# Attention and two feed-forward layers on one core: seven gelus on one engine, and a maximum over tokens in three operations

## The chip, the cores and the metric

The kernel runs on one core of a Trainium2 chip. The metric is the device time of one execution in microseconds (us). The engines are named as the profile names them: PE is TensorE (matmuls; PEld its weight loads), DVE is VectorE, ACT is ScalarE, POOL is GpSimd, SP is SyncE, which issues the DMAs. Differences of under about 2 us cannot be told from run to run (the three runs shown below spread over 1.45 us).

## What is computed

A linear attention with softmaxes over q's features and over k's tokens, then two feed-forward layers with different activations:

```python
q_s = softmax(q, axis=-1)                 # 4 batches, 8 heads, 576 tokens, 64 features
k_s = np.exp(k - np.max(k, axis=2, keepdims=True))
k_s = k_s / (np.sum(k_s, axis=2, keepdims=True) + 1e-09)
kv = np.einsum('bhsd,bhse->bhde', k_s, v)
x = np.einsum('bhsd,bhde->bhse', q_s, kv)  # -> 2304 tokens x 512
h = x @ w_in                               # 512 -> 2048
g = h * (1.0 / (1.0 + np.exp(-1.702 * h))) # the gelu of this text
x = g @ w_out                              # 2048 -> 512
h = x @ w_in2
out = (h * np.tanh(np.log1p(np.exp(h)))) @ w_out2
```

All matmuls of the feed-forward layers run in a 32-bit format that keeps fewer bits. So each operand is split into a high part (a copy in that format) and a low part (the value less the high part), and every product is made of three matmuls.

## The kernel before

**Tiles and stages.** Tokens come in five blocks (512, 512, 512, 384, 384). The first three blocks of the first layer run as 48 *units*, 16 to a block; unit n is one 128-wide slice of the 2048 hidden features of one block. A unit is 12 matmuls into one of two PSUM banks `h` (`gemm_in`, L938), the gelu (`gelu`, L952 and L957), the split into high and low parts (`gelu_split`, recorded at L352 and L344), and, two units later, 12 matmuls into the four banks `acc` (`gemm_out`, L981). PE's order in a quiet stretch is in(n), out(n-2), in(n+1), out(n-1), and so on. Behind unit 47 comes a second phase, which makes the rest of the first layer and the second layer with fewer, combined matmuls (L1203, L1456, L1561, L1586).

**What runs beside the units.** During block 0 (units 0 to 15) all 32 weight tiles of the first layer are still being made: each is loaded raw by a DMA, scaled twice (L361, on ACT), put together by three operations of DVE (L398, L405, L410), and split (L352, L344). `attention(blk)` makes the input x of a block: `q_soft` is the softmax of q, `k_later` and `k_kv` handle two heads of k and v at a time (four such k units for a batch of tokens), `q_turn` and `x_part` make x itself (L812 on ACT, L817 on DVE write it). `attention(0)` runs first and uses another path for k (`k_first`). `attention(1)` must be done before unit 16, `attention(2)` before unit 32, and `attention(3)`, which needs fresh k units as well, directly behind it. `attention(4)` has no k units.

**The gelu before.** ACT takes tanh(0.851 h) from PSUM into `gt` (L952); DVE adds 1 and multiplies by h (L957), which gives twice the gelu. The bank h is free when L957 has read it. x2_evac multiplies by 0.5 later. Tanh and Exp are in the table of functions that ACT loads at the start (L312), and two more loads come in the second phase (L1224).

**The maximum over tokens before.** `k_max` takes the maximum of a tile of 96 partitions x 768 over its 6 tokens per partition with one reduction (L599), whose input is read with the token as the innermost index, so with a step of 64 elements. PE turns the result over (L603), DVE reduces the rest (L604), PE spreads it over partitions again (L677), DVE subtracts (L679), ACT takes Exp (L680), PE multiplies with v (L693), and ACT scales the result (L721).

**What sets the order.** The kernel first collects all operations with their reads and writes (`plan.op` with keys). A planner then orders them for every engine by urgency and by an estimated cost, and emits them; it also chooses the engine where two can do an operation (`either` is DVE or POOL, `copy` is DVE or ACT). Each engine then runs its own queue strictly in order, and waits for the others by semaphores. So a changed cost or dependency can change any order of the whole program.

Of the kernel before, what the change touches and what calls it, by code (L numbers as in the profile page):

```python
# [210 lines left out]
def tile_attention_moe_moe(  # L211
# [29 lines left out]
    SIZES = (512, 512, 512, 384, 384)  # L241
    NBLK = len(SIZES)
    NDIR = 3
    BEGIN = (None, 2, 18, 26, 34)
    BASE = [sum(SIZES[:t]) for t in range(NBLK + 1)]
    MB = max(SIZES)
    MH = max(SIZES[1::2])
# [40 lines left out]
    ap = actx.enter_context(tc.tile_pool(name="attn", bufs=1))  # L288
    kt = [ap.tile([KP, 2, KC, D], F32, name=f"kt{i}") for i in range(2)]
    qt = ap.tile([P, NCT, 4, D], F32, name="qt")  # L290
    pmt = [ap.tile([KP, P], F32, name=f"pmt{i}") for i in range(2)]
    kv32 = [ap.tile([P, P], F32, name=f"kv32_{i}") for i in range(NHP)]
    qT32 = [ap.tile([P, MB], F32, name=f"qT32_{i}") for i in range(2)]
    mcol = ap.tile([P, NHP], F32, name="mcol")
# [23 lines left out]
    def f32(t):  # L318
        return t.bitcast(F32)
# [10 lines left out]
    def pe(ns, reads, writes, fn, whole=False):  # L330
        plan.op([(PE, ns, fn, whole)], reads, writes)
# [258 lines left out]
    def k_max(u, ps, key):  # L590

        kk = ("kt", k_tile(u))
        t, m, mk = kt[k_tile(u)], mcol[:, u % NHP : u % NHP + 1], ("mc", u % NHP)
        pm, pk = pmt[u % 2], ("pm", u % 2)
        dve(
            768,
            [kk],
            [pk],
            lambda: nc.vector.reduce_max(  # L599
                out=pm.rearrange("p (j d) -> p j d", j=2), in_=t.rearrange("p j c d -> p j d c"), axis=AX.X  # L600
            ),
        )
        pe(110, [pk], [key], lambda: nc.tensor.transpose(ps, pm, ident[0:KP, 0:KP]))  # L603
        dve(96, [key], [mk], lambda: nc.vector.reduce_max(out=m, in_=ps, axis=AX.X))  # L604

    def k_first(u, ps, keys):
# [33 lines left out]
        for i, (lo, hi) in enumerate(TURNS):  # L640
            act(
                (hi - lo) * KP + 150,
                [keys[i], mk],
                [tk + (i,), sk + (i,)],
                lambda i=i, n=(hi - lo) * KP: nc.scalar.activation(
                    out=turned[i], in_=ps[i][:, 0:n], func=AF.Exp, bias=m, accum_out=ks[:, u, i : i + 1]
                ),
                psum=True,
            )
# [23 lines left out]
    def k_later(u, ps1, ps2, key):  # L673
        kk, mk = ("kt", k_tile(u)), ("mc", u % NHP)
        t, m = kt[k_tile(u)], mcol[:, u % NHP : u % NHP + 1]
        k_max(u, ps1[:, 0:KP], key)
        pe(110, [mk], [key], lambda: nc.tensor.transpose(ps2[0:KP, :], m.to_broadcast([P, KP]), ident))  # L677
        far = ps2[0:KP, :].rearrange("p (j o d) -> p j o d", j=2, o=1).to_broadcast([KP, 2, KC, D])
        dve(768, [kk, key], [kk], lambda: nc.vector.tensor_tensor(out=t, in0=t, in1=far, op=ALU.subtract))  # L679
        act(768, [kk], [kk], lambda: nc.scalar.activation(out=t, in_=t, func=AF.Exp))  # L680

    def k_kv(u, ps3, key3):
        first = u < NHP
# [64 lines left out]
    def q_soft(blk, half, begun):  # L748
# [20 lines left out]
        if (blk, half) in GROUPS:  # L769

            dve(NQ, [sk], [sk], lambda: nc.vector.tensor_single_scalar(out=s, in_=s, scalar=-1.0, op=ALU.mult))
            for i in range(NQ):
                act(
                    D + 223,
                    key + [sk],
                    key + [("qsum", half)],
                    lambda i=i: nc.scalar.activation(  # L777
                        out=flat()[:, i],
                        in_=flat()[:, i],
                        func=AF.Exp,  # L780
                        bias=s[:, i : i + 1],
                        accum_out=qsum[0:np_, half, i : i + 1],
                    ),
                )
            dve(NQ, [("qsum", half)], [sk], lambda: nc.vector.tensor_scalar_add(s, qsum[0:np_, half, :], 1e-9))
        else:
            either(n, ALU.subtract, flat, flat, wide, key + [sk], key)
            act(n, key, key, lambda: nc.scalar.activation(out=flat(), in_=flat(), func=AF.Exp))
            dve(n, key, [sk], lambda: nc.vector.reduce_sum(out=s, in_=flat(), axis=AX.X))
            dve(NQ, [sk], [sk], lambda: nc.vector.tensor_scalar_add(s, s, 1e-9))  # L790
        dve(8 * NQ, [sk], [sk], lambda: nc.vector.reciprocal(s, s))
# [140 lines left out]
    def gemm_in(h, hkeys, t, fc, ccs=range(NCC)):  # L932
        buf, nb = t % 2, SIZES[t]
        for cc in ccs:
# [10 lines left out]

            pe(3 * mm_ns(nb), x_keys(buf, cc) + [("W", 0, fc, 0), ("W", 0, fc, 1)], [spine] + hkeys, mm)

    def gelu(n):
        nb = SIZES[n // NFC]
        h = hps[n % 2][:, 0:nb]  # L950
        t, tk, hk = gt[n % 2][:, 0:nb], ("gt", n % 2), ("h", n % 2)
        act(nb, [hk, ("tables",)], [tk], lambda: nc.scalar.activation(out=t, in_=h, func=AF.Tanh, scale=0.851), psum=True)  # L952
        dve(
            nb,
# [5 lines left out]
    def gelu_split(n):  # L960
        nb = SIZES[n // NFC]
        t, tk = gt[n % 2][:, 0:nb], ("gt", n % 2)
        o = g_of(n)
        copy(nb, lambda: o[:, 0, :], lambda: t, [tk], [("g", n % 2, 0)])
        either(
            nb,
# [250 lines left out]
        return t.rearrange("p i a n -> p i (a n)")  # L1217

    def activated(n, j, half, t, tk):
        first = n in (0, NPR) and (j, half) == (0, 0)  # L1220

        def fn():
            if first:
# [454 lines left out]
    for n in range(NS):  # L1678
        t, fc = divmod(n, NFC)
        if n == 0:  # L1680

            gemm_in1(0, range(NCC // 2))
            gemm_in1(1, range(NCC // 2))
        gemm_in1(n, range(NCC) if n >= 2 else range(NCC // 2, NCC))
        gelu(n)
        if n >= 2:
            gemm_out(n - 2)
# [13 lines left out]
                x_split(kk, 0)  # L1701
        if n >= NS - 4 and n < NS:
            ring_load(0, n - NS + 4)
        if n in BEGIN:
            attention(BEGIN.index(n))
        if n == NS - 8:
            plan.op(
# [86 lines left out]
```

## Time and profile before

| | us |
|---|---|
| median of 3 runs | 835.64 |
| lowest and highest | 834.77, 836.22 |
| the profiled execution | 833.88 |
| its span, first to last instruction | 832.1 |

The profiled execution is 1.76 us under the median. PE is busy for 98% of the span, but that share is no measure of its pace: a matmul's record is longer than the step to the next one, and in a stretch with waits or with a lower clock PE looks nearly as busy. The pace is read from the chain of waits: in a quiet stretch 12 matmuls of 128x512 take 2.72 us. DVE and ACT records overlap their neighbours by about 0.08 to 0.1 us, so that the *step* from one to the next of a full engine is the recorded duration less that.

### The profile page before, as it was taken

To read this page: it belongs to the slowest core of one execution; us is meant where nothing else is said; L and a number is where in the kernel's file an instruction comes from. 1 tells how busy PE (TensorE), PEld (TensorE's weight loads), DVE (VectorE), ACT (ScalarE), POOL (GpSimd) and SP (SyncE) were. 2 spreads that over 40 slices of the span, in tenths; PEclk is the share of its full clock that TensorE was granted. 3 is DMA by queue.
4 is the path that set the end of the run, shared out by engine and by line. 5 is a ranking of instruction groups with operands and counts; after the bars stand their busy time and mean duration, and the time that the engine had idled before them with its cause. 6 is when DMAs were issued, how large, how long until landed. Compare 5 with 4: busy or idle time off the path is not lost.

```text
span 832.1 us, 13739 instructions
## 1 busy us (share of the span) xinstructions
PE 817.9 (98%) x4897; PEld 727.2 (87%) x4897; DVE 668.9 (80%) x1247; ACT 459.8 (55%) x916; POOL 17.9 (2%) x22
## 2 busy tenths in 40 slices
PE   8999989999999999999999999999999999999998
PEld 7787767887777887999999988988999999999998
DVE  7999996879998777764779979979587977777964
ACT  6988795335455444643447756448344555344542
POOL 0002100000000000000000000000000002000000
PEclk9999999999999999999999999999999999999999
DMA  9688771634468577766778888978788897588872
GB/s 265 193 247 256 212 233 51 207 115 130 135 198 262 201 241 256 211 220 221 249 240 307 270 256 252 276 233 254 232 289 277 277 367 281 181 263 274 289 240 58
DMA packets 120933, 191.75 MB, mean 230 GB/s; under 512 B 36897, under 2 KB 85281, under 8 KB 120865
## 3 DMA queue, kind: packets, MB, share of 16 engines
q1 hardware_dynamic: 120864, 190.88, 72.7%
q8 instruction: 39, 0.64, 0.3%
q14 instruction: 30, 0.24, 0.1%
HBM read 137.89 MB, written 52.95 MB: 229 GB/s over the span
## 4 chain that ended last, share of the span: by engine, by line
PE 82%; DVE 8%; ACT 4%; DMA 4%; issue 1%; SPq 1%; DVEq 0%; ACTq 0%
PE at L1203 21%; PE acc L1456 14%; PE acc L981 11%; PE h L938 10%; PE h L1203 7%; PE acc L1586 5%; PE acc L1561 5%; PE h L1586 3%; PE h L1561 3%; DMA raw<-in_moe_w_in_dram 1%; DMA raw<-in_moe_w_out_dram 1%; DVE pmt L599 1%; PE at L857 1%; DVE dec L410 1%; ACT qt L777 1%
## 5 line engine op out<-in xcount | busy, mean ns | idle before, releaser
L938 PE MATMUL h<-xt,wi 128*128 128x512 f32 x576 | 147.6, 399 | 1.4 <-DVE gt L957 0.9
L981 PE MATMUL acc<-g,wo 128*128 128x512 f32 x576 | 147.2, 400 | 0.4 <-ACT stage L801 0.4
L1203 PE MATMUL at<-xt,wi 128*128 128x384 f32 x732 | 144.4, 335 | 0.1
L1203 PEld LDWEIGHTS at<-xt,wi 128*128 128x128 f32 x732 | 128.8, 188 | 6.4 <-DVE quad L1255 0.4
L938 PEld LDWEIGHTS h<-xt,wi 128*128 128x128 f32 x576 | 106.0, 188 | 26.0 <-DVE gt L957 1.3
L981 PEld LDWEIGHTS acc<-g,wo 128*128 128x128 f32 x576 | 107.0, 189 | 24.0 <-ACT stage L801 0.8
L1456 PE MATMUL acc<-wi,second 128*128 128x256 f32 x738 | 91.0, 283 | 0.0
L1456 PEld LDWEIGHTS acc<-wi,second 128*128 128x128 f32 x738 | 89.7, 192 | 0.0
L1225 ACT ACTIVATE quad<-quad 128x384 f32<-128x384 f32 x64 | 33.6, 526 | 66.4 <-DVE quad L1255 62.6
L352 ACT ACTIVATE second<-quad 128x384 fp32r<-128x384 f32 x84 | 43.9, 524 | 38.1 <-PE acc L1456 35.2
L344 DVE TENSOR_TENSOR second<-quad,second 128x384 fp32r<-128x384 f32 x84 | 46.6, 557 | 16.5 <-ACT second L352 16.3
L1203 PE MATMUL at<-wi,wi 128*128 128x384 f32 x294 | 58.3, 335 | 0.0
L352 ACT ACTIVATE g<-gt 128x512 fp32r<-128x512 f32 (+1 forms) x52 | 32.2, 620 | 38.1 <-PE acc L981 29.1
L1203 PEld LDWEIGHTS at<-wi,wi 128*128 128x128 f32 x294 | 51.9, 188 | 1.6 <-ACT stage L801 0.2
L952 ACT ACTIVATE gt<-h 128x512 f32<-128x512 f32 x48 | 28.6, 595 | 36.6 <-PE h L938 34.0
L1255 DVE TENSOR_TENSOR stage<-at,stage 128x384 f32<-128x384 f32 x58 | 31.9, 552 | 20.7 <-PE at L1203 20.6
L361 ACT ACTIVATE dec<-raw 128x512 f32<-128x512 f32 x62 | 41.5, 669 | 12.0 <-DMA raw<-in_moe_w_out_dram 6.0
L1225 ACT ACTIVATE stage<-stage 128x384 f32<-128x384 f32 x47 | 24.6, 523 | 40.3 <-DVE stage L1255 40.2
L957 DVE SCALAR_TENSOR_TENSOR gt<-gt,h 128x512 f32<-128x512 f32 x48 | 32.7, 681 | 15.2 <-ACT gt L952 15.2
L344 DVE TENSOR_TENSOR g<-gt,g 128x512 fp32r<-128x512 f32 (+1 forms) x49 | 33.0, 674 | 14.6 <-ACT g L352 14.6
L405 DVE SCALAR_TENSOR_TENSOR dec<-raw,dec 128x512 int32<-128x512 int32 x64 | 43.9, 687 | 0.5
L410 DVE CUSTOM_DVE_ANT_0 dec<-raw,dec 128x1024 uint16<-128x1024 uint16 x64 | 43.7, 683 | 0.6
(187 smaller groups left out, 1400.3 us busy)
## 6 DMA issues: line engine op xcount, KB each, us to landing
wi<-combos SPq DMA_DIRECT2D x96, 512.0 KB, 4.5
wi<-outs SPq DMA_DIRECT2D x48, 512.0 KB, 5.7
raw<-in_moe_w_in_dram SPq DMA_DIRECT2D x32, 512.0 KB, 5.0
raw<-in_moe_w_out_dram SPq DMA_DIRECT2D x32, 512.0 KB, 4.7
combos<-raw SPq DMA_DIRECT2D x32, 512.0 KB, 3.7
wi<-combos SPq DMA_DIRECT2D x32, 256.0 KB, 4.9
outs<-raw SPq DMA_DIRECT2D x32, 256.0 KB, 4.3
combos<-raw SPq DMA_DIRECT2D x24, 256.0 KB, 4.3
```

Of the source, the lines that this page charges most:

```text
L344: return lambda: engine.tensor_tensor(out=out(), in0=in0(), in1=in1(), op=op)
L352: (ACT, act_ns(n), lambda: nc.scalar.activation(out=out(), in_=in_(), func=AF.Copy), False),
L361: (ACT, act_ns(512), lambda: nc.scalar.activation(out=out, in_=in_, func=AF.Copy, scale=scale), False),
L405: lambda: nc.vector.scalar_tensor_tensor(out=a, in0=hi_w, scalar=-0x80000000, in1=a, op0=ALU.bitwise_and, op1=ALU.bitwise_or),
L410: dve(512, [rl], [da], lambda: nc.vector.tensor_tensor(out=a, in0=a, in1=lo_w, op=ALU.add), pair=True)
L938: nc.tensor.matmul(out=h(), lhsT=w_mm(fc, 0, a, cc), rhs=x_of(t)[:, cc, b, :], start=cc == 0 and i == 0, stop=cc == NCC - 1 and i == 2,)
L981: nc.tensor.matmul(out=acc[dm][:, 0:nb], lhsT=w_mm(fc, 1, a, dm), rhs=g_of(n)[:, b, :], start=fc == 0 and i == 0, stop=fc == NFC - 1 and i ...
L1203: nc.tensor.matmul(out=bank_of(key)[:, 0:NB], lhsT=wt(fc, 0)[:, w : w + P], rhs=operand(k, b)[:, cc, :], start=cc == 0 and i == 0, stop=cc ...
L1225: nc.scalar.activation(out=t(), in_=t(), func=AF.Mish if n >= NPR else AF.Gelu_apprx_sigmoid)
L1456: nc.tensor.matmul(out=bank_of(banks[c])[:, at_ : at_ + 256], lhsT=slot(pr, a)[:, c * P : c * P + P], rhs=rhs(b), start=pr == 0 and i == 0 ...
L1561: nc.tensor.matmul(out=bank_of(out_banks[c]), lhsT=g_tile(n, j)[:, a, c * P : (c + 1) * P], rhs=w_mm(2 * pr + j, 1, b, 0, 512), start=pr = ...
L1586: nc.tensor.matmul(out=o, lhsT=w_mm(2 * n + j, 1, a, dm), rhs=g_tile(n, j)[:, b, lo:hi], start=n == 0 and j == 0 and i == 0 and (c < 4 or ...
```

## The change

Four edits go together.

1. For units 0 to 6 (`direct(n)`: n < 7; the other bound, 48, is past the last unit) the gelu is one operation of ACT (Gelu_apprx_sigmoid) from PSUM into `gt`, and DVE's L957 is gone. The doubling goes into the split: the high part is ACT's copy with scale 2.0 (it can no longer go to DVE), the low part is one operation of DVE, 2 x gelu less the high part (it can no longer go to POOL).
2. That function is in another table than Exp and Tanh. So there is a table load on ACT before gelu(0) and one back before gelu(7). Every Exp and Tanh reads the key `tables`, and so stays on its side of the loads.
3. `attention(1)` is collected at unit 7, behind the second load, and no longer at unit 2, since its Exps need the first table.
4. `k_max`: the strided reduction gives way to a two-input maximum of tokens 0 to 2 with tokens 3 to 5 (96 x 384) and two more of 96 x 128 each, all with contiguous runs of 64. There is one buffer `pmt` of three parts in place of two.

```diff
-    BEGIN = (None, 2, 18, 26, 34)
+    BEGIN = (None, 7, 18, 26, 34)
+    NEAR, NFAR = 7, 48
...
-    pmt = [ap.tile([KP, P], F32, name=f"pmt{i}") for i in range(2)]
+    pmt = ap.tile([KP, 3, P], F32, name="pmt")
...
-        pm, pk = pmt[u % 2], ("pm", u % 2)
+        pk = ("pm", 0)
         dve(
-            768,
+            384,
             [kk],
             [pk],
-            lambda: nc.vector.reduce_max(
-                out=pm.rearrange("p (j d) -> p j d", j=2), in_=t.rearrange("p j c d -> p j d c"), axis=AX.X
+            lambda: nc.vector.tensor_tensor(
+                out=pmt.rearrange("p c (j d) -> p j c d", j=2), in0=t[:, :, 0:3, :], in1=t[:, :, 3:6, :], op=ALU.max
             ),
-        )
-        pe(110, [pk], [key], lambda: nc.tensor.transpose(ps, pm, ident[0:KP, 0:KP]))
+            pair=True,
+        )
+        for c in (1, 2):
+            dve(
+                P,
+                [],
+                [pk],
+                lambda c=c: nc.vector.tensor_tensor(out=pmt[:, 0, :], in0=pmt[:, 0, :], in1=pmt[:, c, :], op=ALU.max),
+                pair=True,
+            )
+        pe(110, [pk], [key], lambda: nc.tensor.transpose(ps, pmt[:, 0, :], ident[0:KP, 0:KP]))
...
-        act(768, [kk], [kk], lambda: nc.scalar.activation(out=t, in_=t, func=AF.Exp))
+        act(768, [kk, ("tables",)], [kk], lambda: nc.scalar.activation(out=t, in_=t, func=AF.Exp))
...
+    def direct(n):
+        return n < NEAR or n >= NFAR
+
+    def table(name):
+        plan.op([(ACT, 1283.0, lambda: nc.scalar.preload_act_table_set(name), False)], [], [("tables",)])
+
     def gelu(n):
...
+        if direct(n):
+            act(nb, [hk, ("tables",)], [tk], lambda: nc.scalar.activation(out=t, in_=h, func=AF.Gelu_apprx_sigmoid), psum=True)
+            return
...
+        if direct(n):
+            act(
+                nb,
+                [tk],
+                [("g", n % 2, 0)],
+                lambda: nc.scalar.activation(out=o[:, 0, :], in_=t, func=AF.Copy, scale=2.0),
+            )
+            dve(
+                nb,
+                [tk, ("g", n % 2, 0)],
+                [("g", n % 2, 1)],
+                lambda: nc.vector.scalar_tensor_tensor(
+                    out=o[:, 1, :], in0=t, scalar=2.0, in1=f32(o[:, 0, :]), op0=ALU.mult, op1=ALU.subtract
+                ),
+                pair=True,
+            )
+            return
...
+        if NEAR and n in (0, NEAR):
+            table("exp_and_others" if n else "gelu_apprx_sigmoid_and_others")
+        if n == NFAR:
+            table("gelu_apprx_sigmoid_and_others")
+        if n in BEGIN and n == NEAR:
+            attention(BEGIN.index(n))
         gelu(n)
...
-        if n in BEGIN:
+        if n in BEGIN and n != NEAR:
             attention(BEGIN.index(n))
```

The planner orders everything anew. Three places show what stands in the queues. The line numbers of the changed kernel differ: L812, L952, L777, L599 and L604 of before are L822, L971, L787, L600 to L610 and L614 there; L969 and L988 are the new gelu and the new copy, L962 is the table load. In the names, a number is a buffer.

ScalarE, from the second half of x of block 0 (`xt`) to the gelu of unit 0. Before:

```order
L812 ACTIVATE xt<-at_111 128x512
L352 ACTIVATE wi_70<-dec_94 128x512
L812 ACTIVATE xt<-at_112 128x512
L361 ACTIVATE raw_88<-raw_88 128x512
L361 ACTIVATE raw_89<-raw_89 128x512
L361 ACTIVATE dec_94<-raw_89 128x512
L352 ACTIVATE wo_81<-dec_92 128x512
L952 ACTIVATE gt<-h_106 128x512
```

Now:

```order
L822 ACTIVATE xt<-at_111 128x512
L962 ACT_TABLE_LOAD
L822 ACTIVATE xt<-at_112 128x512
L362 ACTIVATE dec_93<-raw_88 128x512
L353 ACTIVATE wi_70<-dec_94 128x512
L362 ACTIVATE raw_88<-raw_88 128x512
L362 ACTIVATE raw_89<-raw_89 128x512
L969 ACTIVATE gt<-h_106 128x512
```

The load stands between the two last pieces of x of block 0, and two weight operations (`dec_93`, `wi_70`) that stood ahead of the second piece of x stand behind it.

ScalarE, up to the first Exps of `attention(1)` (`qt,qsum`). Before, with unit 8's gelu (L952):

```order
L361 ACTIVATE raw_89<-raw_89 128x512
L352 ACTIVATE g<-gt 128x512
L361 ACTIVATE dec_92<-raw_90 128x512
L361 ACTIVATE raw_90<-raw_90 128x512
L952 ACTIVATE gt<-h_106 128x512
L361 ACTIVATE raw_91<-raw_91 128x512
L777 ACTIVATE qt,qsum<-qt,qs 128x64
```

Now, from unit 6's gelu (L969) to unit 7's (L971):

```order
L969 ACTIVATE gt<-h_106 128x512
L962 ACT_TABLE_LOAD
L353 ACTIVATE wo_82<-dec_93 128x512
L787 ACTIVATE qt,qsum<-qt,qs 128x64
L362 ACTIVATE dec_92<-raw_91 128x512
L988 ACTIVATE g<-gt 128x512
L362 ACTIVATE raw_91<-raw_91 128x512
L362 ACTIVATE dec_93<-raw_88 128x512
L353 ACTIVATE wi_76<-dec_94 128x512
L787 ACTIVATE qt,qsum<-qt,qs 128x64
L971 ACTIVATE gt<-h_107 128x512
```

The Exps now begin behind unit 6's gelu and the load, two units earlier than before, and are mixed with the weight operations of those units.

VectorE, the maximum of the second k unit of `attention(1)` (its tile is `kt_117`). Before:

```order
L713 TENSOR_SCALAR rs<-at_111 128x1
L599 TENSOR_REDUCE pmt_120<-kt_117 96x128
L714 RECIPROCAL rs<-rs 128x1
L410 ISA dec_93<-raw_89,dec_93 128x1024
L768 TENSOR_REDUCE qs<-qt 128x16
```

Now:

```order
L600 TENSOR_TENSOR pmt<-kt_117 96x2x3x64
L723 TENSOR_SCALAR rs<-at_111 128x1
L778 TENSOR_REDUCE qs<-qt 128x16
L724 RECIPROCAL rs<-rs 128x1
L781 TENSOR_SCALAR qs<-qs 128x16
L610 TENSOR_TENSOR pmt<-pmt 96x128
L345 TENSOR_TENSOR g<-gt,g 128x512
L610 TENSOR_TENSOR pmt<-pmt 96x128
```

Three shorter operations stand in place of one, and other work of the queue stands between them.

## Rows read from the trace of the kernel before

**Rows 1.** Chain of waits, 136 to 142 us: start, us, what.

```profile
136.86 2.72 PE h L938 x12
```

**Rows 2.** Stretches: window, length, busy us per engine (instructions), clock, DMA share, GB/s.

```profile
37.00:70.00 33.00, 33.00 (x148) 27.30 (x147) 32.64 (x58) 27.14 (x48) 4.71 (x2) 1.00 0.86 256
70.00:133.00 63.00, 58.33 (x328) 43.58 (x327) 61.50 (x114) 52.33 (x145) 4.34 (x4) 0.97 0.64 196
...
180.00:260.00 80.00, 78.04 (x519) 60.00 (x518) 68.97 (x126) 42.59 (x86) 1.45 (x2) 1.00 0.55 161
```

**Rows 3.** Waits of DVE, 37 to 133 us (total, times, longest); first of three.

```profile
DVE g L344 <- ACT g L352: 0.7, 1, 0.7
```

**Rows 4.** Waits of PE, 180 to 262 us; the first two of four.

```profile
PE at L603 <- ACT kv L721: 0.8, 3, 0.3
PE at L827 <- DVE xt L817: 0.6, 1, 0.6
```

**Rows 5.** Waits of PE, 24 to 38 us; the first of two.

```profile
PE h L938 <- DVE gt L957: 0.9, 1, 0.9
```

**Rows 6.** Waits of PE, 70 to 135 us; the first four of six.

```profile
PE at L827 <- DVE qt L344: 1.5, 2, 1.0
PE at L857 <- ACT qT L837: 1.1, 1, 1.1
PE at L693 <- ACT kt L680: 0.9, 1, 0.9
PE at L677 <- DVE mcol L604: 0.7, 1, 0.7
```

**Rows 7.** Smaller stretches, columns as in rows 2.

```profile
92.00:94.00 2.00, 2.00 (x6) 1.43 (x6) 2.00 (x5) 1.61 (x3) 0.00 (x0) 0.50 0.18 39
...
75.00:90.00 15.00, 13.66 (x61) 10.68 (x60) 15.00 (x29) 15.00 (x46) 1.34 (x1) 1.00 0.85 254
90.00:105.00 15.00, 14.03 (x79) 10.89 (x79) 14.30 (x25) 9.61 (x21) 1.29 (x1) 0.89 0.64 176
105.00:120.00 15.00, 13.55 (x97) 10.12 (x97) 14.89 (x27) 14.96 (x51) 1.51 (x1) 1.00 0.74 241
```

**Rows 8.** Timeline of PE, 88 to 94 us: start, us, instructions [idle before <-releaser].

```profile
88.48 0.66 PE L827 MATMUL at<-ident,qt 128*128 128x128 f32 x4 [0.47 <-DVE qt L344]
90.22 0.43 PE L857 MATMUL at<-qT,kv 128*128 128x64 f32 x2 [1.09 <-ACT qT L837]
90.47 3.60 PE L981 MATMUL acc<-g,wo 128*128 128x512 f32 x9
```

**Rows 9.** Timeline of all engines, 31.5 to 37.9 us.

```profile
34.20 0.68 DVE L957 SCALAR_TENSOR_TENSOR gt<-gt,h 128x512 f32<-128x512 f32 x1
...
34.80 0.68 DVE L410 CUSTOM_DVE_ANT_0 dec<-raw,dec 128x1024 uint16<-128x1024 uint16 x1
```

**Rows 10.** Groups of DVE by form: count | busy us, mean ns | idle before.

```profile
L957 DVE SCALAR_TENSOR_TENSOR gt<-gt,h 128x512 f32<-128x512 f32 x48 | 32.7, 681 | 15.2 <-ACT gt L952 15.2
L599 DVE TENSOR_REDUCE pmt<-kt 96x128 f32<-96x768 f32 x12 | 18.3, 1526 | 0.0
L817 DVE TENSOR_TENSOR xt<-at,xt 128x384 fp32r<-128x384 f32 x4 | 2.2, 546 | 0.0
L817 DVE TENSOR_TENSOR xt<-at,xt 128x128 fp32r<-128x128 f32 x4 | 1.1, 278 | 0.0
L768 DVE TENSOR_REDUCE qs<-qt 96x16 f32<-96x1024 f32 x4 | 4.8, 1209 | 0.0
```

**Rows 11.** Timeline of ACT at its last table load.

```profile
460.36 1.28 ACT L1224 ACT_TABLE_LOAD   x1
462.20 0.53 ACT L1225 ACTIVATE stage<-stage 128x384 f32<-128x384 f32 x1 [0.55 <-DVE stage L1255]
```

**Rows 12.** ACT: a group to 345 us (as rows 10); a line's ns least/median/most.

```profile
L361 ACT ACTIVATE dec<-raw 128x512 f32<-128x512 f32 x39 | 26.2, 672 | 2.3 <-DMA raw<-in_moe_w_out_dram 1.6 <-DMA raw<-in_moe_w_in_dram 0.5
...
L777 ACT ACTIVATE qt<-qt,qs x32: 331/335/358, 72.6 to 116.4; 128x64 f32<-128x64 f32 x32
```

More of the change, by code (lines that the diff above doesn't have):

```diff
@@ L642, in k_first @@
                 (hi - lo) * KP + 150,
-                [keys[i], mk],
+                [keys[i], mk, ("tables",)],
                 [tk + (i,), sk + (i,)],
@@ L774, in q_soft @@
                     D + 223,
-                    key + [sk],
+                    key + [sk, ("tables",)],
                     key + [("qsum", half)],
@@ L787, in q_soft @@
             either(n, ALU.subtract, flat, flat, wide, key + [sk], key)
-            act(n, key, key, lambda: nc.scalar.activation(out=flat(), in_=flat(), func=AF.Exp))
+            act(n, key + [("tables",)], key, lambda: nc.scalar.activation(out=flat(), in_=flat(), func=AF.Exp))
             dve(n, key, [sk], lambda: nc.vector.reduce_sum(out=s, in_=flat(), axis=AX.X))
@@ L1219, in activated @@
     def activated(n, j, half, t, tk):
-        first = n in (0, NPR) and (j, half) == (0, 0)
+        first = n in ((0, NPR) if NFAR >= NS else (NPR,)) and (j, half) == (0, 0)
         def fn():
```

## The prediction

> **What bounds the kernel now.** PE has work for nearly the whole span, so only what keeps it waiting or slow can be won. First its pace: in a quiet stretch 12 matmuls of 128x512 take 2.72 us [rows 1]. Then the stretches [rows 2]. From 37 to 70 us PE has no idle time, and DVE is busy for 32.64 of 33 us: DVE just keeps up. From 70 to 133 us, where `attention(1)` comes on top of the last weights, DVE is busy for 61.5 of 63 us and waits for almost nothing (its longest wait is 0.7 us [rows 3]), while PE idles for 4.7 us. From 180 to 260 us (`attention(2)` and `attention(3)`) DVE is at 68.97 of 80 us, no longer full, and PE idles for 2.0 us [rows 4], the two waits left out there being 0.4 and 0.2.
>
> Who ends PE's waits? In the start, one of 0.9 us: unit 2's matmuls wait for bank h, which L957 frees on DVE [rows 5]. From 70 to 135 us, DVE ends 2.2 and ACT 2.0 of the 4.2 us shown [rows 6]; the two left out are 0.3 and 0.2. The smaller stretches say that ACT has its share: from 75 to 90 and from 105 to 120 us, where the Exps of the two softmaxes of q stand, ACT is as full as DVE (15.00 and 14.96 of 15 us), and between these it idles [rows 7]. One more cost hangs on the waits: behind PE's idle times up to 90.22 us [rows 8] the granted clock is 0.50 in the stretch 92 to 94 us [rows 7], TensorE's lower level, 1.2 GHz, and nine matmuls take 3.60 us [rows 8] where 9/12 of 2.72 is 2.04: some 1.5 us lost.
>
> So what the change can win is bounded: 0.9 in the start, 4.7 + 1.5 in `attention(1)`, 2.0 in the next two, 9.1 us in all. Behind 262 us PE's view of waits has no entry, and the order of PE's matmuls in the second phase is the same in both kernels, so I put nothing there.
>
> **The change, part by part.** A queue that is full moves by steps, which are recorded durations less the overlap: L957 starts at 34.20, the next at 34.80 [rows 9], a step of 0.60 for a record of 0.68.
>
> *Gelu.* Seven L957 leave DVE: 7 x 0.60 = 4.2 us. The new gelu stands where the tanh stood on ACT; the trace has no such gelu out of PSUM with 128x512, and I price it as the tanh, which reads the same number of elements from the same place, so at no difference (0.1 us either way would be 0.7 us on ACT). The high part was ACT's copy in these units before, and still is. The low part is a three-input form like L957 in place of a two-input one like L817; both have a step of 0.60 at 512 elements, so nothing. But three low halves that POOL made before 133 us (of its six instructions there [rows 2]) come back to DVE: +3 x 0.60 = +1.8. A few choices between engines go both ways in the new order (a weight half leaves DVE, a copy of k comes): -0.1.
>
> *Maximum over tokens.* L599 takes 1.53 us, a step of 1.45 [rows 10]. In its place stand a two-input maximum of 96x384, whose nearest row is L817 at 128x384, 0.546, step 0.47, and two of 96x128, nearest L817 at 128x128, 0.278, step 0.20 [rows 10]. Together 0.87, so 0.58 us less for each k unit. From one side: with no overlap the three take 0.55 + 2 x 0.28 = 1.11 against 1.53, a gain of 0.42. From the other: were the short ones half as dear, 0.67, a gain of 0.78. Four units in `attention(1)` give 2.3 us (1.7 to 3.1), the eight later ones 4.6 (3.4 to 6.2).
>
> Why the old one is dear stands beside it: the contiguous reduction of 96x1024 takes 1.21 us [rows 10], so 768 elements would take 0.9; the strided one takes 1.53. The Trainium skill, VectorE: DVE Perf Modes, section "Mode 1× (REGULAR) — the baseline", says that in this mode odd strides all work, at one result a cycle; by that the reduction was near 0.9 us and three operations would win nothing, the sum below losing its parts of 2.3 and 1.6. Row and page differ, and the row decides.
>
> *Table loads.* Two more on ACT, 1.28 us each; at the last one of before, the next activation starts 1.84 us after the load does, with 0.55 of that put down to a wait for DVE [rows 11]. So a switch costs 1.28 to 1.84 us; I take 1.28, since the rest has a waiter's name. The Trainium skill, ScalarE: Activation LUTs, section "What ACT_TABLE_LOAD costs", puts a drain on top and 2.66 us in all on a switch; by that the sum below would be 1.4 us worse. The trace here has no switch that long.
>
> *What is queued behind them.* The first load stands between the two last pieces of x of block 0, which PE needs for units 0 and 1. In turn two weight operations that stood ahead of the second piece now stand behind it (one L361, 0.67 [rows 12], and one copy of the same size, about 1.1 in steps), and a copy of k has gone to DVE. So I cost the load at nothing in the start; uncovered it is 1.28. The second stands behind gelu(6), in front of the first Exps. I count it in full, since the engine behind it is full in the Exps' stretches.
>
> *attention(1) at unit 7.* It costs nothing: its first Exp ran at 72.6 us before [rows 12], behind gelu(8), and the new place allows it behind gelu(6), two units earlier.
>
> *The one buffer pmt.* PE reads it right after it is made, and the next k unit's maximum comes after this unit's subtraction and Exp: nothing, or a wait of DVE for PE's short transposition.
>
> **The sum**, against the profiled execution's own 833.88 us:
> - start: the ACT operation alone frees the bank, without L957: -0.9 (with the load uncovered, +0.4).
> - `attention(1)`: DVE is relieved by 4.2 + 2.3 - 1.8 + 0.1 = 4.8, of which 1.2 (gelu 0 and 1) lies in the start. So -3.6 on a full DVE, and +1.3 for the second load on an ACT that is full half the time: -2.3.
> - `attention(2)` and (3): of PE's 2.0 us of waits, those on L721, L817 and the 0.2 on L680, 1.6 us, hang on the chain of maximum, subtraction, Exp and scaling, which gets 0.58 shorter eight times: -1.6.
> - together -4.8, so 829.1 for that execution. It stood 1.76 under the median of the runs, and the median is what I forecast: 835.64 - 4.8 = **830.8 us**.
>
> **The rivals.**
> - *DVE's relief comes through whole.* The Exps move to where ACT had gaps, the load is hidden, the waits in (2) and (3) all go, and so does the slow clock: -0.9 - 3.6 - 2.0 - 1.5 = -8.0, 827.6. For it: ACT's idle time from 90 to 105 us [rows 7]. Against it: a full ACT in both stretches of Exps.
> - *ACT takes the place of DVE.* ACT ends PE's waits in `attention(1)` as often as DVE [rows 6]; if it sets the end there, nothing is won there, and in the later stages only a part: -0.9 - 0.6 = -1.5, 834.1.
> - *Slower.* The first load lies on the way of block 0's x (+0.4 with the wait that goes); the second takes 1.84, and with the Exps behind it makes the gelus of units 7 to 10 late, so that PE waits for a bank and the clock falls once more (1.5): 0.4 + 1.84 + 1.5 - 1.6 = +2.1, 837.7. From gelu(6) to gelu(8) ACT's new queue holds seven Exps (0.33 each), 14 weight and copy operations (0.55), two gelus (0.5) and the load: 12.3 us, against 4 x 2.72 = 10.9 on PE. So a gelu falls 1.4 us behind; it decides from where this passes the three groups, 8.2 us, that PE has between a unit and the next one on its bank. That is far off.
> - *The relief is there and is not used.* The changed costs reorder every queue, and the work comes back elsewhere: within 1.5 us of before.
>
> **How the numbers follow.** Forecast 0.40 (a gain of 3.0 to 6.5), whole relief 0.22 (6.5 to 9.1, or some more with a better clock), ACT 0.22 (0 to 3.0), slower 0.09, unused 0.07. About 0.2%, 1.7 us, is what can be told from no change. Faster by that: 0.40 + 0.22 + 0.10 of ACT's case = 0.72; within: 0.12 + 0.06 = 0.18; slower: 0.09 + 0.01 = 0.10. The range is 826.0 to 835.4: it leaves out some 0.05 below, where all waits are gone and the clock is better too, and some 0.12 above, the slower case and the edges of the two small ones.
>
> **What would show it.** In the changed profile: PE's wait on L957 in the start gone, and no wait of over 0.3 us for the second piece of x; the maxima at about 0.55, 0.28 and 0.28 us; DVE still full while `attention(1)` runs, and PE's waits there near half; the clock at 1.00 throughout only in the case of the whole relief; from 180 to 260 us PE's waits under 0.6 us. The forecast would be wrong if ACT is full from 60 us to the end of `attention(1)`, if PE waits for a gelu or a tanh of units 7 to 10, or if PE's waits show entries behind 262 us.

## The result, and the profile after

| | before | after |
|---|---|---|
| median, first comparison, us | 835.24 (4 runs) | 826.45 (4 runs) |
| ratio, with its 95% interval | | 0.9904 [0.9891, 0.9918] |
| median, repeated beside experiments, us | 834.10 (10 runs) | 826.49 (6 runs) |
| ratio, with its 95% interval | | 0.9911 [0.9895, 0.9928] |
| profiled execution, us | 833.88 | 827.49 |

The changed kernel is faster by 7.6 to 8.8 us, 0.9 to 1.0%. The forecast was 830.8; its range, 826.0 to 835.4, holds the time, but the gain is nearly twice the 4.8 us of the sum, and the rival that nearly met it is "DVE's relief comes through whole" (827.6). The two profiled executions differ by 6.4 us only: that of before stands under its median, that of after is the longest of its four.

The page of the changed kernel, its span, PE's share and the granted clock in 40 slices:

```profile
span 825.7 us, 13769 instructions
PE 815.2 (99%) x4893; PEld 728.4 (88%) x4893; DVE 662.2 (80%) x1266; ACT 462.5 (56%) x918; POOL 14.4 (2%) x20
PEclk9999999999999999999999999999999999999999
```

The three stretches of [rows 2], with the same columns:

```profile
37.00:70.00 33.00, 33.00 (x147) 27.36 (x146) 32.96 (x63) 30.56 (x61) 0.00 (x0) 1.00 0.83 256
70.00:133.00 63.00, 59.46 (x345) 45.65 (x344) 57.63 (x116) 52.53 (x138) 3.14 (x2) 1.00 0.66 196
180.00:260.00 80.00, 79.49 (x526) 62.40 (x525) 70.65 (x147) 45.22 (x88) 3.51 (x2) 1.00 0.58 175
```

DVE (third pair) is as full from 37 to 70 us as it was. From 70 to 133 us it went from 61.50 to 57.63 of 63 us: it now has room. PE idles there for 3.5 us against 4.7, and from 180 to 260 us for 0.5 against 2.0.

PE's waits in the changed kernel (line waited for: total, times, longest), from 24 to 38 us, 70 to 135 us and 170 to 262 us, which answer to [rows 5], [rows 6] and [rows 4]:

```profile
PE h L948 <- DVE xt L827: 0.2, 1, 0.2
PE h L948 <- ACT xt L822: 0.2, 1, 0.2
```

```profile
PE at L837 <- DVE qt L345: 2.1, 1, 2.1
PE at L613 <- ACT kv L731: 0.8, 1, 0.8
PE at L687 <- DVE mcol L614: 0.5, 1, 0.5
PE h L948 <- DVE xt L827: 0.2, 1, 0.2
```

```profile
PE acc L1017 <- ACT stage L811: 0.5, 1, 0.5
```

In the start the wait for L957 is gone. In the middle stage four waits are left, 3.6 us in all, where six made 4.7; the longest, 2.1 us, is for `qt`, which the split of q's softmax on DVE ends. In the last, only a wait outside the chain of the maximum is left.

The new operations, by form on DVE (L600 and L610, the three maxima) and on ACT (L969, the gelu), count | busy us, mean ns:

```profile
L610 DVE TENSOR_TENSOR pmt<-pmt 96x128 f32<-96x128 f32 x24 | 6.7, 278 | 0.0
L600 DVE TENSOR_TENSOR pmt<-kt 96x384 f32<-96x384 f32 x12 | 6.5, 545 | 0.0
```

```profile
L969 ACT ACTIVATE gt<-h 128x512 f32<-128x512 f32 x7 | 4.2, 596 | 0.4 <-PE h L948 0.2
```

A clean account by stage needs marks on PE that both orders share: unit 2's first matmul, the first of unit 12's and of unit 31's second product (`gemm_out`), the second phase's first. Stretches between the first three of these marks, of before and then of after, columns as above; the first holds most of `attention(1)`, the second its last k units and most of `attention(2)` and (3). They are called the first and the second stage below:

```profile
34.93:115.72 80.79, 77.14 (x370) 61.07 (x371) 79.62 (x141) 68.09 (x169) 7.54 (x4) 0.98 0.77 228
115.72:248.09 132.37, 129.77 (x767) 101.31 (x766) 111.65 (x201) 66.24 (x130) 2.96 (x3) 1.00 0.48 147
```

```profile
34.35:111.58 77.23, 74.63 (x371) 59.88 (x371) 75.51 (x147) 71.76 (x176) 3.14 (x2) 1.00 0.82 242
111.58:241.26 129.68, 128.74 (x770) 102.03 (x768) 108.03 (x219) 66.74 (x127) 3.51 (x2) 1.00 0.49 151
```

So the start gains 0.58 (34.93 to 34.35), the first stage 3.56, the second 2.69; what is behind gives 0.44 back (span 832.10 less 248.09, against 825.71 less 241.26). In the second stage PE's idle time shrinks by 1.66 (2.60 to 0.94), and the time in its records by 1.03 although there are three more of them, so idle time alone does not hold the whole gain.

The two executions differ in one more thing: the first stage of before holds a stretch at the low clock [rows 7], that of after does not. A second profiled execution of the changed kernel (`e9_after_again`) has one at the same place. Its two stages:

```profile
33.01:111.32 78.31, 76.04 (x372) 61.35 (x372) 75.93 (x147) 71.84 (x176) 3.53 (x2) 0.98 0.80 242
111.32:241.00 129.68, 128.73 (x770) 102.05 (x768) 108.05 (x219) 66.70 (x127) 3.51 (x2) 1.00 0.49 149
```

Like for like, then, the first stage gains 2.48 (80.79 to 78.31), and the second again 2.69.

### The profile page after: what moved, and what is told of

Its sections match the earlier page's. It is cut to its first block, busy times and chain, and to the rows that moved or that the text cites. A ratio compares the mean times of both kernels' runs of the same rounds, so it can differ in the third digit from the quotient of the medians.

```text
span 825.7 us, 13769 instructions
## 1 busy us (share of the span) xinstructions
PE 815.2 (99%) x4893; PEld 728.4 (88%) x4893; DVE 662.2 (80%) x1266; ACT 462.5 (56%) x918; POOL 14.4 (2%) x20
## 4 chain that ended last, share of the span: by engine, by line
PE 88%; DVE 5%; ACT 3%; DMA 2%; issue 1%; SPq 0%
PE at L1239 21%; PE acc L1492 14%; PE acc L1017 13%; PE h L948 13%; PE h L1239 7%; PE acc L1597 5%; PE acc L1622 5%; PE h L1597 3%; PE h L1622 2%; PE at L867 2%; PE at L703 1%; DVE dec L411 1%; PE acc L627 1%; DMA raw<-in_moe_w_in_dram 1%; PE at L837 1%
## 5 line engine op out<-in xcount | busy, mean ns | idle before, releaser
L353 ACT ACTIVATE g<-gt 128x512 fp32r<-128x512 f32 (+1 forms) x45 | 27.8, 619 | 38.3 <-PE acc L1017 33.8
L345 DVE TENSOR_TENSOR g<-gt,g 128x512 fp32r<-128x512 f32 (+1 forms) x45 | 30.2, 672 | 17.1 <-ACT g L353 16.9
L1239 PE MATMUL h<-xt,wi 128*128 128x384 f32 x228 | 43.2, 334 | 0.0
L345 DVE TENSOR_TENSOR quad<-quad 128x384 f32<-128x384 f32 x64 | 35.4, 556 | 9.4 <-ACT quad L1261 8.3
```

Of the source, the lines that this page charges most:

```text
L345: return lambda: engine.tensor_tensor(out=out(), in0=in0(), in1=in1(), op=op)
L353: (ACT, act_ns(n), lambda: nc.scalar.activation(out=out(), in_=in_(), func=AF.Copy), False),
L1239: nc.tensor.matmul(out=bank_of(key)[:, 0:NB], lhsT=wt(fc, 0)[:, w : w + P], rhs=operand(k, b)[:, cc, :], start=cc == 0 and i == 0, stop=cc ...
```

## The experiments

Two theories stood at the beginning. **A**: the work that DVE is rid of sets the time, and its parts add up. **B**: the new order of the queues brings the gain, and the work taken off hardly matters by itself. Since the planner sets the order from costs and dependencies, both can be held apart: a kernel can keep the order of one version and emit the work of the other. Lines of the diffs stand against the changed kernel, unless it says otherwise. Times are ratios to the kernel before, run beside the experiments (medians 834.0, 833.2 and 834.1 us in three groups); each has at least six runs.

### Each part alone, ordered anew

`e1_gelu_only` has edits 1 to 3 of the change, `e2_max_only` edit 4.

In `e1_gelu_only`:

```diff
-            lambda: nc.vector.tensor_tensor(
-                out=pmt.rearrange("p c (j d) -> p j c d", j=2), in0=t[:, :, 0:3, :], in1=t[:, :, 3:6, :], op=ALU.max
+            lambda: nc.vector.reduce_max(
+                out=pm.rearrange("p (j d) -> p j d", j=2), in_=t.rearrange("p j c d -> p j d c"), axis=AX.X
```

In `e2_max_only`:

```diff
-    BEGIN = (None, 7, 18, 26, 34)
-    NEAR, NFAR = 7, 48
+    BEGIN = (None, 2, 18, 26, 34)
...
-        if direct(n):
-            act(nb, [hk, ("tables",)], [tk], lambda: nc.scalar.activation(out=t, in_=h, func=AF.Gelu_apprx_sigmoid), psum=True)
-            return
```

> The change's gelu part alone (direct gelu for units 0 to 6, both table loads, attention(1) at unit 7), with the strided maximum of before, ordered anew by the planner. Theory A (VectorE's relief sets the time, the two parts add): VectorE loses 4.2 us less 1.8 that come back from GpSimd, the start gains 0.6 as in the changed kernel, the later attentions nothing: 835.2 - 3.0 = 832.2 us. Theory B (the gain is that of the new order, with the Exps of attention(1) two units earlier and no slow clock, and hardly that of the work itself): most of the gain stands already here, 828 us or less.

> The three-operation maximum alone, in the kernel of before, ordered anew. Theory A: 12 x 0.58 = 7.0 us less on VectorE, of which 2.3 in attention(1), where it is full, and up to 2.7 in the next two, as the changed kernel won there: 835.2 - 5.0 = 830.2 us. Theory B: without the earlier Exps little in attention(1): 833 us or more.

Measured: 0.9992 [0.9980, 1.0005] and 0.9961 [0.9948, 0.9974]: -0.7 and -3.3 us, together -3.9, half of what both bring at once. The first can't be told from nothing, and misses the 832.2 of theory A as it does the 828 of theory B; the second meets theory A. The gelu alone wins 2.39 us in the first stage (78.40 us) and takes 3.21 more in the second (135.58); but in this execution the second holds the matmuls of one more k unit (24), and the stretch at the low clock, which costs 1 to 1.5 us by an estimate from the last section. Effects that add up, theory A's second half, are out.

### The new order without one part of the relief

`e3_order_strided` keeps the changed kernel's order and puts the one strided reduction back in the place of the three operations. `e4_order_tanh` keeps the order and puts tanh and DVE's operation back; both added loads stay, of the table already there.

In `e3_order_strided`:

```diff
-            lambda: nc.vector.tensor_tensor(
-                out=pmt.rearrange("p c (j d) -> p j c d", j=2), in0=t[:, :, 0:3, :], in1=t[:, :, 3:6, :], op=ALU.max
+            lambda: nc.vector.reduce_max(
+                out=pmt[:, 0, :].rearrange("p (j d) -> p j d", j=2), in_=t.rearrange("p j c d -> p j d c"), axis=AX.X
...
-                lambda c=c: nc.vector.tensor_tensor(out=pmt[:, 0, :], in0=pmt[:, 0, :], in1=pmt[:, c, :], op=ALU.max),
+                lambda: None,
```

In `e4_order_tanh`:

```diff
-            act(nb, [hk, ("tables",)], [tk], lambda: nc.scalar.activation(out=t, in_=h, func=AF.Gelu_apprx_sigmoid), psum=True)
+            def both():
+                nc.scalar.activation(out=t, in_=h, func=AF.Tanh, scale=0.851)
+                nc.vector.scalar_tensor_tensor(out=t, in0=t, scalar=1.0, in1=h, op0=ALU.add, op1=ALU.mult)
+            act(nb, [hk, ("tables",)], [tk], both, psum=True)
...
-            table("exp_and_others" if n else "gelu_apprx_sigmoid_and_others")
+            table("exp_and_others")
```

> The changed kernel with every engine's order kept, but the maximum is again the one strided reduction, at the place of the first of the three operations (the other two are left out). So only the 0.58 us of work in each of 12 k units comes back. Theory A: +2.3 in attention(1) and +2.7 in the next two: 826.5 + 5.0 = 831.5 us. Theory B: the order holds the gain: +1.5 us at most, 828.

> The changed kernel with every engine's order kept, but units 0 to 6 again take the tanh on ScalarE and the add-and-multiply on VectorE, which stands in VectorE's queue where the new gelu stands in ScalarE's; both table loads stay, of the same table. So 7 x 0.60 = 4.2 us of VectorE come back, and in the start the wait for it. Theory A: +0.6 to 0.9 in the start and +3 in attention(1): 826.5 + 3.7 = 830.2 us. Theory B: +1.5 us at most, 828.

Measured: 0.9970 [0.9962, 0.9979] and 0.9976 [0.9965, 0.9987]. Against the changed kernel's 0.9904 to 0.9911 either costs 5 to 6 us, far over the 1.5 us that theory B allowed. So at this order the work does matter, and the two reliefs act at different places. Without the short maxima the second stage takes 132.96 us where the changed kernel takes 129.68; in it PE (first pair) idles 2.79 us against 0.94, as much as before the change:

```profile
112.02:244.98 132.96, 130.17 (x770) 101.61 (x768) 112.92 (x201) 66.67 (x127) 3.11 (x2) 1.00 0.48 147
```

Without the gelu on ACT that stage keeps its gain (129.72), and the first loses all of it: 82.49, with a stretch at the low clock in it, so 4.18 over the 78.31 of the changed kernel's execution that has one too. There `e3_order_strided`, also with one, takes 78.97. PE's waits in `e4_order_tanh` from 24 to 135 us, four of seven; L972 is DVE's gelu operation, put back:

```profile
PE at L837 <- DVE qt L345: 2.2, 1, 2.2
PE acc L1022 <- DVE g L999: 1.4, 2, 1.2
PE h L948 <- DVE wi L345: 0.8, 2, 0.7
...
PE h L948 <- DVE gt L972: 0.6, 1, 0.6
```

All four are ended by DVE. The first stands in the changed kernel too (2.1); the other three, 2.8 us together, do not: in this order, DVE with the old work is late.

### The relief without the new order

`e7_old_order_max` has the order of before, and the three operations where the reduction stood. `e8_old_order_gelu` has the order of before, the gelu as one operation of ACT for units 0 to 6, nothing in the place of L957, and the loads before gelu(0) and gelu(7). The diffs are against the kernel before; `three` issues the three maxima.

```diff
-            lambda: nc.vector.reduce_max(
-                out=pm.rearrange("p (j d) -> p j d", j=2), in_=t.rearrange("p j c d -> p j d c"), axis=AX.X
-            ),
+            three,
```

```diff
+            if n in (0, 7):
+                nc.scalar.preload_act_table_set("exp_and_others" if n else "gelu_apprx_sigmoid_and_others")
+            if n < 7:
+                nc.scalar.activation(out=t, in_=h, func=AF.Gelu_apprx_sigmoid)
...
-            lambda: nc.vector.scalar_tensor_tensor(out=t, in0=t, scalar=1.0, in1=h, op0=ALU.add, op1=ALU.mult),
+            lambda: None if n < 7 else nc.vector.scalar_tensor_tensor(out=t, in0=t, scalar=1.0, in1=h, op0=ALU.add, op1=ALU.mult),
```

> The kernel of before with its order kept, and the three operations in place of the strided reduction (one buffer). Relief alone, at the old order: theory A, as the runs on the changed order said: attention(1) +0 to -1, the next two -3: 834.0 - 3.5 = 830.5 us. Theory B, that it takes the new order to use the relief: 833 or more.

> The kernel of before with its order kept; units 0 to 6 take the gelu in one operation of ScalarE at the tanh's place, VectorE's add-and-multiply is left out there, and the two table loads stand in front of gelu(0) and of gelu(7). The doubling of these units is left out, so their share of the output is half. Relief alone at the old order, 4.2 us of VectorE: theory A: start -0.6 and attention(1) -3 to -4.5 with the slow clock gone: 834.0 - 4.5 = 829.5 us. Theory B (the old order holds the Exps of attention(1) behind gelu(8), so that VectorE is early and nobody uses it): 833 us or more.

Measured: 0.9994 [0.9979, 1.0008] and 1.0001 [0.9989, 1.0013]. Neither kernel can be told from the one before: the relief by the maximum, in the old order, is worth nothing that can be measured, nor is that by the gelu together with its two loads. PE's waits from 70 to 135 us in `e7_old_order_max` (the first four of five) are those of [rows 6], nearly number by number, and in `e8_old_order_gelu` they are much the same (the first two of five):

```profile
PE at L833 <- DVE qt L344: 2.1, 2, 1.6
PE at L863 <- ACT qT L843: 1.1, 1, 1.1
PE at L699 <- ACT kt L686: 0.9, 1, 0.9
PE at L683 <- DVE mcol L610: 0.6, 1, 0.6
```

```profile
PE at L827 <- DVE qt L344: 1.5, 2, 1.1
PE at L857 <- ACT qT L837: 1.2, 1, 1.2
```

In the latter the first load isn't covered as it is in the changed kernel. It stands right in front of gelu(0), and in the start PE's only wait, for the bank that this gelu frees, is longer than the 0.9 for DVE before (24 to 38 us; L957 is the new gelu in this kernel):

```profile
PE h L938 <- ACT gt L957: 1.1, 1, 1.1
```

Where did DVE's 4.2 us go? Into waits of its own. DVE's three longest entries there, 37 to 133 us; before, the longest was 0.7 [rows 3]:

```profile
DVE g L344 <- ACT g L352: 2.4, 2, 1.7
DVE wo L344 <- ACT wo L352: 1.4, 3, 0.7
DVE wi L344 <- ACT wi L352: 0.7, 1, 0.7
```

All three are for ACT's copies. ACT also has the two loads here, 2.6 us, so this run doesn't tell whether ACT's old order or its longer queue makes DVE wait, nor what the gelu's relief would bring at this order with the loads hidden. From 105 to 120 us ACT is as full in it as in [rows 7] (14.96 of 15); in the changed kernel it is not (13.82):

```profile
105.00:120.00 15.00, 13.00 (x96) 9.70 (x95) 14.89 (x28) 14.96 (x50) 1.49 (x1) 1.00 0.67 223
```

```profile
105.00:120.00 15.00, 14.22 (x87) 10.72 (x86) 13.97 (x33) 13.82 (x37) 0.00 (x0) 1.00 0.83 258
```

The Exps of q's softmaxes run from 61.6 to 109.3 us in the changed kernel, from 72.7 to 116.1 in the old order (`e7_old_order_max`).

### What the two table loads cost

`e5_order_no_loads` emits nothing for the loads and tanh for the gelu, all else as in the changed kernel; `e6_order_loads_twice` loads a table twice at both places; `e12_no_loads_again` is the first once more, beside `e9_after_again`, the changed kernel itself.

Without the loads:

```diff
-        plan.op([(ACT, 1283.0, lambda: nc.scalar.preload_act_table_set(name), False)], [], [("tables",)])
+        plan.op([(ACT, 1283.0, lambda: None, False)], [], [("tables",)])
...
-            act(nb, [hk, ("tables",)], [tk], lambda: nc.scalar.activation(out=t, in_=h, func=AF.Gelu_apprx_sigmoid), psum=True)
+            act(nb, [hk, ("tables",)], [tk], lambda: nc.scalar.activation(out=t, in_=h, func=AF.Tanh), psum=True)
```

With two more:

```diff
+        def twice():
+            nc.scalar.preload_act_table_set("exp_and_others" if name[0] == "g" else "gelu_apprx_sigmoid_and_others")
+            nc.scalar.preload_act_table_set(name)
```

> The changed kernel with every engine's order kept, without the two added table loads; units 0 to 6 take a tanh of h where the gelu stood (same engine, size and place), so the activation function of these units is another one. The prediction's step (the second load costs its 1.3 us in full on a full ScalarE): 1.3 us less than the changed kernel, and the first load nothing: 825.1 where the changed kernel stands at 826.4. The rival (ScalarE's gaps hide both): within 0.5 us of the changed kernel.

> The changed kernel with every engine's order kept, and each of the two added table loads issued twice (first the other table, then the right one): 2.6 us more on ScalarE. If the loads are paid in full: +2.6, 829 us; if the first is covered in the start and the second paid: +1.3; if ScalarE has room for both: within 0.5 us of the changed kernel.

> The changed kernel, unaltered, beside the three kernels of this call. It came out at 0.9904 of the kernel before. Both theories expect 0.990 again, within 0.002; it is the basis for the others.

> The changed kernel without its two added table loads, in the same order, now beside the changed kernel on the same chip (units 0 to 6 go through tanh instead of the gelu, and their share of the output is another). If the loads are hidden: within 0.5 us of the changed kernel. If the second stands in the way as the sum had it: 1.3 us under it; if the first does too: 2.6 us.

Measured: without the loads 0.9911 [0.9891, 0.9931] and 0.9913 [0.9896, 0.9930], the changed kernel beside the second 0.9911 [0.9895, 0.9928]. No gain shows; but the intervals, some 1.6 us to either side, hardly exclude the 1.3 us that the prediction charged. The traces are sharper. Without the loads the first stage takes 77.03 us in both profiled executions, against 77.23 with them (all three without a stretch at the low clock), so the second load costs about 0.2 us there. The first leaves PE a wait of 0.2 us for x. The loads are hidden, both of them. With two more, 0.9957 [0.9941, 0.9974], some 4 us slower, more than the 2.6 us of the loads themselves: the cover is used up. The first stage takes 78.52, and in the start the doubled load shows as a wait of PE for the second piece of x, which is 0.2 us in the changed kernel (`e6_order_loads_twice`, PE's waits from 24 to 135 us, the second entry):

```profile
PE h L948 <- ACT xt L822: 1.5, 1, 1.5
```

### One unit more or less

With the loads and the reliefs settled, the last question was whether a better number than seven exists, and whether a unit more brings the 0.6 us that it takes off DVE.

In `e10_near6` (`e11_near8` has 8 at both places):

```diff
-    BEGIN = (None, 7, 18, 26, 34)
-    NEAR, NFAR = 7, 48
+    BEGIN = (None, 6, 18, 26, 34)
+    NEAR, NFAR = 6, 48
```

> The changed kernel with six units instead of seven on one operation of ScalarE, and attention(1) collected one unit earlier. Theory A (the work that VectorE is rid of sets the time, by amounts that add): one scaling less leaves VectorE, 0.60 us, so +0.6 us against the changed kernel. Theory B (what counts is that the queues, arranged anew, have no gap on TensorE; the amount of work taken off hardly matters as such): it depends on how this order falls, not on the 0.6: anything from 0 to +4 us, and where it is over +2 the profile shows a new wait of TensorE or a stretch at a clock of 0.50 between 70 and 133 us.

> The changed kernel with eight units instead of seven on one operation of ScalarE, and attention(1) collected one unit later. Theory A (the work taken off VectorE adds up): a further 0.60 us off, so -0.6 us against the changed kernel, unless ScalarE becomes full. Theory B (the order decides): 0 to +4 us; the Exps of attention(1) come one unit later, behind gelu(7), and where that crowds them, waits for ScalarE or the low clock come back between 90 and 133 us.

Measured: 0.9925 [0.9908, 0.9941] with six, which can't be told from seven, and 0.9949 [0.9931, 0.9967] with eight: 3.3 us slower where the work alone says 0.6 faster. Its waits of PE from 70 to 135 us, the first five:

```profile
PE acc L1017 <- DVE wo L345: 0.9, 1, 0.9
PE at L867 <- ACT qT L847: 0.7, 1, 0.7
PE h L948 <- ACT xt L822: 0.6, 1, 0.6
PE at L837 <- DVE xt L827: 0.6, 1, 0.6
PE at L867 <- DVE xt L827: 0.5, 1, 0.5
```

The long wait for `qt` is gone, and a row of others stands in its place. They do not hold the whole loss: against the changed kernel's first profiled execution the two stages take 0.56 and 0.71 us more (77.79 and 130.39), and what is behind 1.27. No version beat the changed kernel.

**What follows from all.** Neither theory stands alone. One relief in the old order: 0 (two kernels, one of them with the loads). The new order without one of the reliefs: half of the gain or less. Each part ordered anew: -0.7 and -3.3. Both, ordered anew: -7.6 to -8.8. So the gain takes the work and the order together. Two kernels were not run: both reliefs in the old order, and the new order with neither. So it is not shown how far the two reliefs help each other without a new order, nor what the order brings by itself. And since one unit more, ordered anew, costs 3.3 us, part of the gain may lie in how this one order happens to fall.

## Why the prediction came out as it did

**Prices.** The three maxima were put at 0.55 + 2 x 0.28 from the nearest rows [rows 10] and take 0.545 and 0.278; the gelu was priced as the tanh, whose group has 594 ns in the changed kernel, and takes 596. That the strided reduction was dear for its stride was a reading of rows [rows 10]; by the rule of the Trainium skill cited there ("VectorE: DVE Perf Modes", section "Mode 1× (REGULAR) — the baseline"), as the prediction read it, the maximum should have won nothing. `e2_max_only`, 3.3 us faster, and `e3_order_strided`, 5 us slower than the changed kernel, speak for the rows.

**Start, -0.9.** The wait on L957 went, as said, and with DVE's operation put back in the new order it is there again at 0.6 (`e4_order_tanh`). The mark stands 0.58 us earlier; but in the other profiled execution of the changed kernel it stands at 33.01, 1.92 earlier, and in two executions of one kernel without the loads at 32.64 and 35.19. So one execution of each doesn't give this term to better than 2.5 us. The first load at nothing: right, with 0.2 us of wait left and little more room, as the doubled load shows.

**`attention(1)`, -2.3.** The first stage gained 3.56 between the first two profiles, but like for like, with the stretch at the low clock in both, 2.48. So the size was nearly right, and that is in part luck, since two errors cancel. The first is the second load, +1.3 "in full": it is hidden. It starts at 59.78 and the next activation runs 1.30 us later (timeline of ACT):

```profile
59.17 0.60 ACT L969 ACTIVATE gt<-h 128x512 f32<-128x512 f32 x1
59.78 1.28 ACT L962 ACT_TABLE_LOAD   x1
61.08 0.63 ACT L353 ACTIVATE wo<-dec 128x512 fp32r<-128x512 f32 x1
```

ACT is full in the Exps' stretches, the argument went; but the load stands ahead of these, where ACT had 5.9 us of idle time in 33 (27.14 busy [rows 2]; 30.56 now). I charged the load at the fullness of a stretch in which it doesn't lie. By the rule of the Trainium skill ("ScalarE: Activation LUTs", section "What ACT_TABLE_LOAD costs") a switch takes 2.66 us with its drain. These lines show 1.30, and the gelu in front ends where the load starts, so they show no drain on either side of it. The second error is the relief, -3.6 "on a full DVE": with the load at nothing, some 2.5 of it arrived by these marks. DVE was expected to be still full here and PE's waits near half; DVE is at 57.63 of 63 us, and the waits went from 4.7 to 3.6. Which wait holds back the rest is not shown. ACT does not take DVE's place: it ends one PE wait of 0.8 us, where it ended 2.0 us before [rows 6]. With both loads covered, the slower rival had nothing to stand on.

**`attention(2)` and (3), -1.6.** The mechanism was right, as `e3_order_strided` and `e4_order_tanh` show: the maximum carries the second stage, and the gelu has no part in it. In `e2_max_only`, without the gelu, the stage takes 128.02. The size was bounded by PE's idle time in the view of waits, 2.0 [rows 4], and the stage, which also holds the end of `attention(1)`, gained 2.69, of which 1.03 lies in the records themselves. The bound was none.

**Behind 262 us, 0.** A wait of 0.3 us for ACT is new there, which the prediction had named as a sign of being wrong; the stretch behind unit 31's mark is 0.44 us longer in the one execution of after and 0.18 shorter in the other. Neither can be told from nothing.

**Where the excess lies.** The second execution of the changed kernel stands 7.3 us under the one of before, where the sum had 4.8. Of the 2.5 between them the second stage has 1.1, the start 1.0 (within its scatter), the first stage and what is behind 0.2 each.

**The choice among the cases.** The whole relief had 0.22, my forecast 0.40. What spoke "against it", a full ACT in both stretches of Exps, was a state of the old order, and the new one spread the Exps (13.82 of 15 us where it was 14.96). Of that rival's four conditions the spread Exps and the hidden load came true, and the waits of (2) and (3) went but for one of 0.5. The fourth, the slow clock gone, did not hold: four of ten executions of the changed kernel have it (below). So its 827.6 came nearest, but not by its own account. Both cases counted DVE's relief as if it moved PE by itself, and the order as a risk only ("the relief is there and is not used", 0.07). In the old order that is what happens: the relief is there and isn't used.

## What to carry to other kernels

Where several engines run in-order queues that wait for each other, taking work off the fullest one can be worth nothing until the order is made anew, and two reliefs together can be worth twice their sum; so try them together before dropping one that brought nothing alone. Charge an added operation at the fullness of the engine in the stretch where it will stand, not of the busiest stretch near it. PE's idle time in the view of waits can fall short of what waits cost it; marks on its own matmuls, with equal work between them, give the whole. Profile the same kernel twice before crediting a stage with its difference.

## What the runs showed of the hardware

**The low clock comes in some executions of a kernel only.** The prediction held the stretch at 1.2 GHz behind `attention(1)`'s waits [rows 7] for a cost of those waits, about 1.5 us. It is not there in the changed kernel's first profiled execution, and is there in its second (`e9_after_again`), at the same place and behind the same wait, of 2.07 and of 2.09 us. One stretch of 3.4 us from the end of that wait in the first, and in the second that one and one that begins 1.1 us later (the clock is the third number from the end):

```profile
83.00:86.40 3.40, 3.35 (x18) 2.81 (x19) 3.40 (x4) 2.84 (x6) 1.51 (x1) 1.00 0.63 219
```

```profile
81.70:85.10 3.40, 3.37 (x13) 2.85 (x14) 3.40 (x5) 2.85 (x6) 1.53 (x1) 0.67 0.62 205
82.80:86.20 3.40, 3.40 (x11) 2.74 (x10) 3.40 (x5) 2.85 (x7) 0.62 (x1) 0.50 0.63 202
```

Behind the same wait PE gets 18 matmuls through in the one and 13 in the other. Between these two executions the first stage differs by 1.08 us (77.23 and 78.31). The mean granted clock of an execution tells whether it had such a stretch: in the 14 profiled ones it is 0.997 or 0.998 with one and 1.000 without. By that, 20 of 62 executions of the kernel before had it, with a median of 834.46 us against 833.19; of ten of the changed kernel four, with the same median as the others within 0.1 us. So the stretch goes with 1 to 1.5 us, near what the prediction had, yet it comes in a third of the executions of before only. The order has a share in it: of `e2_max_only`, `e10_near6` and `e11_near8` none of 18 executions has it. What decides it among the executions of one kernel, no run here shows. An edit can't be credited with its absence in one profile.

**A reduction with a step of 64 elements takes DVE about two thirds longer.** The reduction of 96x768 with that step takes 1526 ns, a contiguous one of 96x1024 1209 [rows 10], which is 907 for 768 elements by proportion, an estimate. The two differ in the length of their groups as well: six elements go into each result of the first, 64 into each of the second. No run tells the step's part from that of the short groups.
